# An attention and maxout kernel on one core: two bursts of ones resized and the engines' order searched anew

## The chip, the cores and the metric

The kernel runs on one core of one Trainium2 chip. A core has a matrix engine (TensorE, PE in the profile; its weight loads are PEld), a vector engine (DVE), an activation engine (ACT), a general engine (POOL) and an engine that issues transfers (SP), each with its own queue of instructions that it works off in order. They meet through semaphores alone. The metric is the device time of one execution in microseconds; lower is better.

## What is computed

Queries, keys and values have 8 batches, 8 heads, 1152 positions and 64 channels. Neighbouring queries are averaged in pairs, then comes plain softmax attention, and its output, 4608 tokens of 512 channels, goes through a maxout layer:

```python
q_pool = q.reshape(B, H, S // 2, 2, D).mean(axis=3)
scores = np.matmul(q_pool, k.transpose(0, 1, 3, 2)) / np.sqrt(D)
attn = np.exp(scores - scores.max(-1, keepdims=True))
attn = attn / (attn.sum(-1, keepdims=True) + 1e-09)
x = np.matmul(attn, v).transpose(0, 2, 1, 3).reshape(B * S // 2, H * D)
out = np.maximum(x @ w1, x @ w2) @ w_out
```

## The kernel before

**How the work is cut.** Two heads of one batch make a pair; there are 32 pairs, numbered in order of batch, four to a batch. The scores of all pairs are one long row of 324 groups of 512 columns (`scores`, L665). Each group is computed for both heads at once: a head has 64 channels, so its product uses 64 of the array's 128 rows, and the products of the two heads lie side by side. ACT turns a group into exponentials (L672). A pair's attention times values is a set of products with all 128 rows: first a block of half width for the last 64 queries (L588), then four blocks of nine products for each head (L576). A column of ones next to the values gives the sum of the softmax, so that the normalization is one reciprocal (L598) and two multiplications (L602, L606) on DVE.

The normalized output is transposed, mostly by transfers that SP issues (L712), into `xT`, channels by tokens, in four quarters of the channels, one for each pair of a batch. The maxout layer uses max(a, b) = relu(a - b) + b: the hidden layer (`h_pairs`, L864) multiplies `xT` by w1 - w2 and is cut off at zero by DVE (L874), and the output layer (`p_pair`, L897) adds that times w_out to `xT` times the product of w2 and w_out, which is made once. Both layers use 64-row products in pairs, too. Three forms of product therefore follow each other on TensorE: 64 rows by 128 columns of the array (scores, both layers), 128 by 128 (L576, transposes), and 128 by 64 (L588).

**What sets the order.** The whole program is recorded as a plan of operations with their reads and writes. Five strings give the order on the engines, one character an operation. In `pe_order`, S is the next score group, a digit is the next part of the job in that lane, and the letters U, V, y, z, Y, Z are bursts of products of ones, which compute nothing. `dve_order`, `act_order`, `pool_order` and `sp_order` do the same for the other engines. Whatever the strings say, each operation waits for what it reads and for the buffer that it writes. After score group 21 the scores alternate between two PSUM buffers, and the third one and `fb` serve all other jobs, so a job's bank must be emptied by DVE before the next job on that bank begins.

**The start.** While the first loads are on their way TensorE multiplies ones (`short`, L406): one burst U and six bursts V, then a burst z (`fill`, L397) and then the first transposes of q (L516) and k (L546). DVE adds the first pairs of q (L471), ACT, DVE and POOL convert k (L454, L456, L458). Bursts Y, of 64 rows and 128 columns, stand among the first score groups.

**Later.** q of a later pair goes from POOL (L477) to eight small transposes on DVE (L533), k from POOL (L444) to a transfer that transposes it (L463).

Of the kernel before, what the change touches and what calls it, by code (L numbers as in the profile page):

```python
# [9 lines left out]
P = 128  # L10
# [277 lines left out]
def bass_funnel_attn__then__act_maxout2_kernel(  # L288
# [14 lines left out]
    HP = P // 2  # L303
# [23 lines left out]
    with outer:  # L327
        def sbuf(shape, dt, name):
            return room.enter_context(nc.sbuf_tensor(name, list(shape), dt))
# [5 lines left out]
        ones_tile = sbuf([P, P], BF16, "warm")  # L335
# [32 lines left out]
        fb = [w[:, half, :] for w in wide for half in range(2)]  # L368
# [4 lines left out]
        def rows(half):  # L373
            return slice(half * HP, half * HP + HP)
# [15 lines left out]
            op("POOL", ones, w=["vE0", "vE1", "vE2"])  # L390
            op("DVE", lambda e: e.memset(ones_tile[:, :], 1.0), w=["warm"])

        def fill(m, z):

            def go(e):
                for _ in range(FILL):
                    last = e.matmul(fb[m][:, 384:512], ones_tile[z, :], ones_tile[z, :],  # L397
                                    start=True, stop=True)
                return last
            return m, go  # L400

        def short(m, count, n):

            def go(e):
                for _ in range(count):
                    last = e.matmul(fb[m][0:HP, 384:384 + n], ones_tile[:, 0:HP], ones_tile[:, 0:n],  # L406
                                    start=True, stop=True)
                return last
            return m, go

        FILL = 4
        fills = {"U": short(0, 8, HP), "V": short(1, 10, 52), "y": fill(0, slice(0, P)), "z": fill(1, slice(0, P)),
                 "Y": fill(0, rows(0)), "Z": fill(1, rows(0))}

        def load_k(i, parts=((0, NT),)):
            b, h0, s = i // NHP, 2 * (i % NHP), i % 3
# [500 lines left out]
        def p_job(lo, tail, c0=0, c1=E):  # L917
# [69 lines left out]
        pe_order = (  # L987
            "VUVVVVVz010SS10SzS0SYYSSYYYY0SSS1Y0zS0SSYSY1S1111SSY0S1S01000S1S0SS0677S77S66S66S7S06S70S67S60S0"
            "677SS666S66S000S77S06S000S006S00S06S66667SS000777S00S60S0060S666S666S6000S000S066S66S660S66S1000"
            "S6S1011S666S66S660S000S6766SS6677S07S000S666S666S6666S66110SS010100S66S6666S60S6606S060S060S0000"  # L990
            "S00S67676SS6677S0000S6S0066S660S6666S000S006S666S60S0000SS1111S666S0000S000S066S66S0000SS11011S6"
            "66S6000S0000S0666S666S666S666S66666S0S0000SS1111S666S6666S000S0066606S00666S6000S06S6666SS7777S0"
            "006666S6660600S60S06666S06666000S6666S66S660S000S06667SS66777S000S6666S66S6600S00S6666SS76777S00"
            "S006S66666S66S6666S0066S666S666S666S600S000S6666SS76777S000S00S6666SS767770SS00600S066S6060S6666"
            "00S00S6666S66006S006S0000S6666S0000SS10111S6666S0000S0000666S011SS010100S666S66S6666S666S6666S66"
            "6S660S000S0667SS667767SS00000S00666S0606666S000S6666S666600S0066S6606666S00S6666SS77767S00S000S0"
            "00000S666SS676777S0S006666S666S60S0000S6666S666S600S000S66S6670SS7677S000S006S606S606S666S0110SS"
            "00110S66S6666S6666S66S666S66666S66S66000S00S6666SS67777S00S00000S000S000S000S000S6666SS67777S000"
            "0S60000666S66660000S00066066S66S606000S00006S666S0011SS01100S666S66S60600S0600S0066S66S0000SS011"
            "11S6S600060S000S06666S60000S0000S66S60S00001111S6S666666S660S6666S6060S60S0000S66666S0000S0S6666"  # L1000
            "6SS77770S0066S66S66606S000S00666SS667777SS00666S666660S66S660S6666S066S666S666000S0S06766SS77766"
            "S0000S000S00S00000006266667577174446533104424371124360241400301226275513623301004202513111022050"
            "011372151226260130600511122002507140521113000113100412002013031231216205302022112211523233353335"
# [90 lines left out]
        def k_cuts(i):  # L1094
            return K0 if i == 0 else (0, 5, 9)

        count = {name: len({j for v in jobs_of.values() for j in v.split() if j.split(".")[0] == name})
                 for name in {j.split(".")[0] for v in jobs_of.values() for j in v.split()}}
# [5 lines left out]
        for c in pe_order:  # L1104
# [7 lines left out]
            elif c in fills:  # L1112
                m, fn = fills[c]
                op("PE", fn, r=["warm"], w=[f"f{m}"])
            else:
                m = int(c)
# [30 lines left out]
        dve(lambda e: e.tensor_reduce(flag[0:1, 0:1], badr[0:1, :], AX.X, ALU.max), ["gr"], ["gd4"])  # L1147

        dve_order = (
            "QQ010Q10Q0W0Q100WW111101W10001W077W66667676766WW6666776T6TT06T66T6T776TTTTTTT6T06TTTT001T1006TTT"  # L1150
            "T66T6677TTT0TTTT1010T00TTTT6TTTTTTT666677T6TT60T0T00011T6TT0TTTT0011006TTTT0TTTTTTTTT00T01T106TT"
            "6TTT66T6677TT66TT6TT06TTT666677T0T6TTTTTT666767T0TT6TTTTTT6TT67667TTTT6666776TTTT60TTT60TTTTT000"
            "01160TTT00TTT110T0TT6TTTTTTT66776666TTT60TTTT667676TTTTTTTTT66667766T0T666677TT0T6T1001TTTTTT0TT"
            "0TTT6T667T6T6T7TTTTTTTT0666677T06T060TTTTTTT010001TT0TTTT000011TTT0T60TTTT000011TTTT06T66T66770T"
            "6TTTT6666770T666667706666770302026025170GGGGG026")
        act_order = (
            "CCSSSSSSSSSSSSSSSSSSSSSSSSSSSSSSSSSSSSSSSSSSSSSSSSSSSSSSSSSSSSSSSSSSSSSSSSSSSSSSSSSSSSSSSSSSSSSS"
# [1 line left out]
            "SSSSSSSSSSSSSSSSSSSSSSSSSSSSSSSSSSSSSSSSSSSSSSSSSSSSSSSSSSSSSSSSSSSSSSSSSSSSSSSSSSSSSSSSSSSSSSSS"  # L1159
            "SSSSSSSSSSSSSSSSSSSSSSSSSSSSSSSSSSSSSSSSSSSSSSSSSS125311102134o6o1oo3o5oo")  # L1160
        pool_order = (
            "ivikkvqkvqkkvdqddvqddkqdddvkqkvkvqkkqqvvqqkvvvqkqkqvkqkvqkvvvkqkkqqvqvkkkkvqqvvqvkvqvkqkvqqkkvqv"
            "kvqqvkkvv")
        sp_order = (
            "qkkqwkqwvwqkwwvwwqkkvwwqwvqqwkvwtkkkqvtqkvttkxxkxqvqtxkvxxqqkqqtvoxvxtvooxvxqtqkvqtokxokotkkxoov"
            "xqtxvvxtqovoxtkoxoxkqokotqtvqkvxkqttqvoxooxqkkxxvtxxotqvqovoxvtkoxxvvoxxtkxoxkoqvoxtxqvqxxotvkto"
# [56 lines left out]
```

## Time and profile before

| | us |
|---|---|
| three runs | 363.45, 367.36, 367.65 |
| their median | 367.36 |
| the profiled execution | 364.59 |
| its span, first to last instruction | 363.3 |
| PE busy | 356.7 |
| ACT busy | 314.8 |
| DVE busy | 242.8 |
| POOL busy | 124.4 |

How to read it: the page of the profile gives busy times and the shares of the chain of work that ended last; the chain of waits lists that chain in order of time; the timeline has one row for equal instructions that follow each other without a gap (start, length, engine, line, operation, tiles, shape, how many, and in brackets the idle time before it and what ended it). Matmuls are pipelined: the length of one covers its way through the array, so rows overlap, and what a product costs is read from the start of its row to the start of the next one. Shapes of TensorE are written rows*columns of the array and then rows x columns streamed.

### The profile page before, as it was taken

To read this page: it belongs to the slowest core of one execution; us is meant where nothing else is said; L and a number is where in the kernel's file an instruction comes from. 1 tells how busy PE (TensorE), PEld (TensorE's weight loads), DVE (VectorE), ACT (ScalarE), POOL (GpSimd) and SP (SyncE) were. 2 spreads that over 40 slices of the span, in tenths; PEclk is the share of its full clock that TensorE was granted. 3 is DMA by queue.
4 is the path that set the end of the run, shared out by engine and by line. 5 is a ranking of instruction groups with operands and counts; after the bars stand their busy time and mean duration, and the time that the engine had idled before them with its cause. 6 is when DMAs were issued, how large, how long until landed. Compare 5 with 4: busy or idle time off the path is not lost.

```text
span 363.3 us, 13386 instructions
## 1 busy us (share of the span) xinstructions
PE 356.7 (98%) x5973; PEld 222.6 (61%) x5973; DVE 242.8 (67%) x528; ACT 314.8 (87%) x355; POOL 124.4 (34%) x111
## 2 busy tenths in 40 slices
PE   8999999999999999999999999999999999999995
PEld 6666666566564666656675665666666556666842
DVE  2577688877589767948968594676976846715421
ACT  4999999989999999999989999999999989894221
POOL 1236896424155322552251612623334420010000
PEclk9999999999999999999999999999999999999998
DMA  7999979999969997995999999998999570823115
GB/s 260 403 398 394 394 173 357 240 266 291 327 149 264 303 266 222 249 251 147 271 342 211 246 305 301 261 225 222 231 283 216 166 159 9 196 44 77 33 32 149
DMA packets 77790, 84.78 MB, mean 233 GB/s; under 512 B 50080, under 2 KB 50848, under 8 KB 77728
## 3 DMA queue, kind: packets, MB, share of 16 engines
q1 hardware_dynamic: 77168, 83.09, 86.9%
q8 instruction: 48, 0.79, 0.9%
q10 hardware_dynamic: 560, 0.79, 0.6%
q14 instruction: 14, 0.11, 0.1%
HBM read 62.91 MB, written 9.44 MB: 199 GB/s over the span
## 4 chain that ended last, share of the span: by engine, by line
PE 94%; ACT 4%; DVE 0%; issue 0%; DVEq 0%
PE sps L665 21%; PE sps L576 13%; PE sps L897 11%; PE fb L897 10%; PE sps L864 9%; PE fb L576 7%; PE fb L864 7%; ACT et L672 4%; PE sps L927 3%; PE sps L588 2%; PE fb L789 2%; PE fb L927 1%; PE sps L837 1%; PE fb L588 1%; PE fb L837 1%; PE fb L406 1%
## 5 line engine op out<-in xcount | busy, mean ns | idle before, releaser
L672 ACT ACTIVATE et<-sps 128x1024 bf16<-128x1024 f32 (+1 forms) x336 | 306.6, 1005 | 19.6 <-PE sps L665 17.6
L665 PE MATMUL sps<-qpT,kT 64*128 64x256 bf16 (+7 forms) x1162 | 120.2, 285 | 0.9 <-DVE qpT L523 0.7
L533 DVE STREAM_TRANSPOSE qpT<-qp 32x288 bf16<-32x288 bf16 x216 | 101.4, 469 | 6.7 <-PE sps L665 1.5
L665 PEld LDWEIGHTS sps<-qpT,kT 64*128 64x128 bf16 x1162 | 47.6, 94 | 49.1 <-ACT et L672 16.2
L477 POOL TENSOR_TENSOR qp<-qraw 128x576 bf16<-128x576 f32 x30 | 42.1, 1406 | 90.3 <-DVE qpT L533 60.5
L483 POOL TENSOR_SCALAR vE<-vraw 128x1152 bf16<-128x1152 f32 x32 | 36.9, 1155 | 69.1 <-DMA vraw<-in_v_dram 66.5
L576 PE MATMUL sps<-vE,et 128*128 128x65 bf16 x1440 | 51.4, 193 | 0.0
L576 PEld LDWEIGHTS sps<-vE,et 128*128 128x128 bf16 x1440 | 46.1, 97 | 7.0 <-issue 6.3
L444 POOL TENSOR_SCALAR kbf<-kraw 128x1152 bf16<-128x1152 f32 x31 | 35.7, 1154 | 30.7 <-DMA kraw<-in_k_dram 15.7
L864 PE MATMUL sps<-xT,wd 64*128 64x512 bf16 (+3 forms) x368 | 43.9, 326 | 0.0
L897 PE MATMUL sps<-wo,stage 64*128 64x512 bf16 x256 | 36.8, 376 | 0.0
L874 DVE TENSOR_SCALAR stage<-sps 128x1024 bf16<-128x1024 f32 (+3 forms) x23 | 22.3, 969 | 17.2 <-PE sps L864 17.0
L864 PE MATMUL fb<-xT,wd 64*128 64x512 bf16 (+3 forms) x272 | 33.5, 333 | 0.1
L897 PE MATMUL fb<-wo,stage 64*128 64x512 bf16 x224 | 33.0, 376 | 0.0
L576 PE MATMUL fb<-vE,et 128*128 128x65 bf16 x864 | 30.3, 193 | 0.0
L576 PEld LDWEIGHTS fb<-vE,et 128*128 128x128 bf16 x864 | 27.4, 97 | 4.1 <-issue 3.2
L874 DVE TENSOR_SCALAR stage<-fb 128x1024 bf16<-128x1024 f32 (+3 forms) x17 | 17.0, 999 | 10.7 <-PE fb L864 10.5
L864 PEld LDWEIGHTS sps<-xT,wd 64*128 64x128 bf16 x368 | 15.6, 94 | 12.9 <-PE sps L864 1.1
L598 DVE RECIPROCAL rcs<-sps 128x4 f32<-128x4 f32 (+1 forms) x40 | 7.4, 185 | 18.3 <-PE sps L576 17.7
L897 PE MATMUL sps<-w,xT 64*128 64x512 bf16 x128 | 18.8, 376 | 0.0
L906 DVE COPY stage<-sps 128x1024 f32<-128x1024 f32 x8 | 9.8, 1225 | 12.8 <-PE sps L897 12.7
L897 PEld LDWEIGHTS sps<-wo,stage 64*128 64x128 bf16 x256 | 12.1, 94 | 9.5
(92 smaller groups left out, 295.0 us busy)
## 6 DMA issues: line engine op xcount, KB each, us to landing
vraw<-in_v_dram SPq DMA_DIRECT2D x32, 576.0 KB, 6.6
kraw<-in_k_dram SPq DMA_DIRECT2D x31, 576.0 KB, 6.0
qraw<-in_q_dram SPq DMA_DIRECT2D x31, 576.0 KB, 7.2
out_dram<-stage SPq DMA_DIRECT2D x21, 256.0 KB, 5.6
out_dram<-stage SPq DMA_DIRECT2D x23, 128.0 KB, 3.6
xT<-in_moe_w_dram SPq DMA_DIRECT2D x4, 512.0 KB, 9.7
stage<-in_moe_w_out_dram SPq DMA_DIRECT2D x4, 512.0 KB, 13.6
stage<-in_moe_w_dram SPq DMA_DIRECT2D x4, 512.0 KB, 13.8
```

Of the source, the lines that this page charges most:

```text
L444: op("POOL", lambda g: g.tensor_scalar(kbf[s][:, :, :, :].rearrange("p t h d -> p h t d"), kraw[r][:, :, :, :], 1.0, 1.0, ALU.mult, ALU.mu ...
L477: op("POOL", lambda g: g.tensor_tensor(qpf[s][:, :, :], qraw[r][:, :, 0, :], qraw[r][:, :, 1, :], ALU.add), r=[f"qraw{r}"], w=[f"qp{s}.0", ...
L483: op("POOL", lambda g: g.tensor_scalar(vE[r][:, :, :, 0:D].rearrange("p t h d -> p h t d"), vraw[r][:, :, :, :], 1.0, 1.0, ALU.mult, ALU.m ...
L533: op("DVE", lambda e: e.transpose(view[dst:dst + 32, :, 32 * pb:32 * pb + 32], qpf[s][src:src + 32, :, 32 * db:32 * db + 32]), r=[f"qp{s}. ...
L576: last = e.matmul(fb[m][:, sb * 66:sb * 66 + 65], et[:, a:a + P], vE[vs][:, t, half, 0:65], start=(t == 0), stop=(t == NT - 1))
L588: last = e.matmul(fb[m][rows(half), NCH * 66:NCH * 66 + 65], et[:, a:a + NB], vE[vs][:, t, half, 0:65], start=(t == 0), stop=(t == NT - 1))
L665: last = e.matmul(sps[r][:, h, col:col + hi - lo], kT[i % 3][rows(h), t, :], qpT[i % 3][rows(h), lo:hi], start=True, stop=True)
L672: op("ACT", lambda e: e.activation(et2[:, :, c:c + z - a], sps[r][:, :, a - g * W:z - g * W], EXP, scale=scale), r=[f"s{r}"], w=keys + ([f ...
L864: last = e.matmul(fb[m + k][:, 0:size], wd[z, ct, (f0 + k) * P:(f0 + k + 1) * P], xT[z, ct, n0:n1], start=(turn == 0 and ct == 0), stop=(t ...
L874: dve(lambda e: e.tensor_scalar_max(gT[:, f0:f0 + 2, g0:g0 + size], wide[m // 2][:, :, 0:size], 0.0), [f"f{m}", f"f{m + 1}"], w + [f"f{m}" ...
L897: last = e.matmul(fb[m + k][:, :], lhs, rhs, start=(turn == 0 and j == 0), stop=(turn == 1 and j == NC_ + NF - 1))
L927: return e.matmul(fb[m][:, 0:c1 - c0], lhs, rhs[:, c0:c1], start=(j == 0), stop=(j == NC_ + NF - 1))
```

## The change

The bursts U and V get other sizes: U was eight products of 64 columns and is ten of 64, each V was ten of 52 columns and is eight of 64. The burst Y was four products of 128 columns and is five of 102. The strings of PE, DVE and POOL are other ones from the second batch to the last. ACT's string is as it was, and SP's is too.

```diff
-        def fill(m, z):
+        def fill(m, z, count=4, n=P):
             def go(e):
-                for _ in range(FILL):
-                    last = e.matmul(fb[m][:, 384:512], ones_tile[z, :], ones_tile[z, :],
+                for _ in range(count):
+                    last = e.matmul(fb[m][:, 384:384 + n], ones_tile[z, :], ones_tile[z, 0:n],
                                     start=True, stop=True)
...
-        def short(m, count, n):
+        def short(m, count):
             def go(e):
                 for _ in range(count):
-                    last = e.matmul(fb[m][0:HP, 384:384 + n], ones_tile[:, 0:HP], ones_tile[:, 0:n],
+                    last = e.matmul(fb[m][0:HP, 384:448], ones_tile[:, 0:HP], ones_tile[:, 0:HP],
                                     start=True, stop=True)
...
-        FILL = 4
-        fills = {"U": short(0, 8, HP), "V": short(1, 10, 52), "y": fill(0, slice(0, P)), "z": fill(1, slice(0, P)),
-                 "Y": fill(0, rows(0)), "Z": fill(1, rows(0))}
+        fills = {"U": short(0, 10), "V": short(1, 8), "y": fill(0, slice(0, P)), "z": fill(1, slice(0, P)),
+                 "Y": fill(0, rows(0), 5, 102), "Z": fill(1, rows(0))}
...
-            "S6S1011S666S66S660S000S6766SS6677S07S000S666S666S6666S66110SS010100S66S6666S60S6606S060S060S0000"
+            "S6S1011S666S6666S0000S0S66666SS7777S00S06666S66S6666S66S6666S1066SS0000S66S111S66S6600S0000S000S"
...
-            "kvqqvkkvv")
+            "vvkqqvkkv")
```

The first operations on TensorE before. `warm` is the tile of ones, and the output size is partitions by columns:

```order
L406 MATMUL fb<-warm 64x52 x10
L406 MATMUL fb<-warm 64x64 x8
L406 MATMUL fb<-warm 64x52 x50
L397 MATMUL fb<-warm 128x128 x4
L516 MATMUL fb<-ident,qp 64x64 x8
```

The same place now (the changed file is one line shorter above, so its line numbers are one less from there on):

```order
L406 MATMUL fb<-warm 64x64 x58
L397 MATMUL fb<-warm 128x128 x4
L515 MATMUL fb<-ident,qp 64x64 x8
L545 MATMUL fb<-ident,kbf 128x128 x4
```

Ten products of ones fewer stand ahead of the first transpose of q.

On TensorE near the 124th score group, where the values of one pair (`vE,et`) stand among scores (`qpT,kT`) and the output layer (`wo,stage`), before:

```order
L897 MATMUL fb<-wo,stage 128x512 x2
L588 MATMUL sps<-vE,et 64x65 x18
L665 MATMUL sps<-qpT,kT 128x448 x2
L665 MATMUL sps<-qpT,kT 128x64 x2
L576 MATMUL sps<-vE,et 128x65 x36
L665 MATMUL sps<-qpT,kT 128x512 x4
L576 MATMUL sps<-vE,et 128x65 x36
L665 MATMUL sps<-qpT,kT 128x64 x2
```

And now:

```order
L587 MATMUL sps<-vE,et 64x65 x18
L896 MATMUL fb<-wo,stage 128x512 x4
L664 MATMUL sps<-qpT,kT 128x448 x2
L664 MATMUL sps<-qpT,kT 128x64 x2
L896 MATMUL fb<-wo,stage 128x512 x4
L664 MATMUL sps<-qpT,kT 128x512 x2
L575 MATMUL sps<-vE,et 128x65 x72
L664 MATMUL sps<-qpT,kT 128x512 x2
```

The 72 products stand in one block in place of two, with scores on both sides and none between. Over the whole program the places where one form of product gives way to another, counted in the order, are 216 before and 211 now.

On DVE, where pair 23 is normalized (`xnat`, from the reciprocals `rcs`), among the transposes of a later pair's q (`qpT`), before:

```order
L598 RECIPROCAL rcs<-sps 128x5
L602 TENSOR_TENSOR xnat<-sps,rcs 64x64
L598 RECIPROCAL rcs<-sps 128x4
L533 STREAM_TRANSPOSE qpT<-qp 32x9x32
L602 TENSOR_TENSOR xnat<-sps,rcs 64x64
L533 STREAM_TRANSPOSE qpT<-qp 32x9x32
L606 TENSOR_TENSOR xnat<-sps,rcs 128x4x64
L533 STREAM_TRANSPOSE qpT<-qp 32x9x32
L606 TENSOR_TENSOR xnat<-sps,rcs 128x4x64
```

And now:

```order
L597 RECIPROCAL rcs<-sps 128x5
L601 TENSOR_TENSOR xnat<-sps,rcs 64x64 x2
L605 TENSOR_TENSOR xnat<-sps,rcs 128x4x64
L532 STREAM_TRANSPOSE qpT<-qp 32x9x32
L597 RECIPROCAL rcs<-sps 128x4
L532 STREAM_TRANSPOSE qpT<-qp 32x9x32 x2
L605 TENSOR_TENSOR xnat<-sps,rcs 128x4x64
```

The first head's part is done in one go, and two transposes of q stand between the second head's reciprocal and its end in place of three. On TensorE, between the last product of that pair (L576) and the first product of the hidden layer that reads its channels (L864), there were 38 products of the output layer (L897), 90 products with values and 10 score groups; there are 24, 90 and 8 now.

More of the change, by code (lines that the diff above doesn't have):

```diff
@@ L989, in bass_funnel_attn__then__act_maxout2_kernel @@
             "677SS666S66S000S77S06S000S006S00S06S66667SS000777S00S60S0060S666S666S6000S000S066S66S660S66S1000"
-            "S6S1011S666S66S660S000S6766SS6677S07S000S666S666S6666S66110SS010100S66S6666S60S6606S060S060S0000"
-            "S00S67676SS6677S0000S6S0066S660S6666S000S006S666S60S0000SS1111S666S0000S000S066S66S0000SS11011S6"
-            "66S6000S0000S0666S666S666S666S66666S0S0000SS1111S666S6666S000S0066606S00666S6000S06S6666SS7777S0"
-            "006666S6660600S60S06666S06666000S6666S66S660S000S06667SS66777S000S6666S66S6600S00S6666SS76777S00"
@@ L994, in bass_funnel_attn__then__act_maxout2_kernel @@
[L994 to L998, printed above, removed]
@@ L999, in bass_funnel_attn__then__act_maxout2_kernel @@
-            "0S60000666S66660000S00066066S66S606000S00006S666S0011SS01100S666S66S60600S0600S0066S66S0000SS011"
-            "11S6S600060S000S06666S60000S0000S66S60S00001111S6S666666S660S6666S6060S60S0000S66666S0000S0S6666"
+            "S6S1011S666S6666S0000S0S66666SS7777S00S06666S66S6666S66S6666S1066SS0000S66S111S66S6600S0000S000S"
+            "000S6S6666SS77770S006S0S06666S606S6600S000S06666S6S00000SS1111S6660S000S00S0066S66S0000SS01111S6"
+            "S66600000S000S666S6666S666S66S666S06S0000SS1111S66S6666S660S0000S6666066S6600S600S00S66667777S0S"
@@ new lines, in bass_funnel_attn__then__act_maxout2_kernel @@
+            "00006666S666600S60S006666S666600S6666S6666S0000S0S66666SS7777S0006S666S66S660000S0S66666SS7777S0"
+            "0S6066S6666S066S666S666S666S666S6066S000S00S6766SS66777S00S000S6660SS667777SS0006S0006S0666S6666"
+            "0S00S06666S666S60000S0000S6666S000001SS11166S660000S000S06666S666S0101SS10100S6S6666S66666S666S6"
+            "6S660S000S6767SS77666S00S006666S66606S000S60666S60666S000S6666060S06660S00S06S6667SS6777S000S000"
+            "S0060SS66667777S0S06666S606S066S0000S006S666S666S60000S0S66677SS7667S0000S000S6660S6S6666S000S6S"
@@ L1001, in bass_funnel_attn__then__act_maxout2_kernel @@
+            "111100S666S66S6666S660S060S666S6666S60S66006S00S000S66676SS07677S00S000S0000S000S66666SS7777S000"
+            "0S00006666S66606000S00006666S66S060060S00006S666S0110SS10001S6S66666S00060S60S6000S6666S0000SS01"
+            "111S66S00600S0000S666S60000S000S0666S66S000100111S66S666S660S6666S6060S60S0000S66666S0000S0S6666"
             "6SS77770S0066S66S66606S000S00666SS667777SS00666S666660S66S660S6666S066S666S666000S0S06766SS77766"
@@ L1149, in bass_funnel_attn__then__act_maxout2_kernel @@
         dve_order = (
[L1150 to L1154, printed above, removed]
+            "QQ010Q10Q0W0Q100WW111101W10001W077W66667676766WW6666776T6TT06T66T6T776TTTTTTT6T06TTTT0011006TTT6"
+            "666T77TT0TTTTTTTTTT000TT101TT6TTTT66T66776TTTTT60TT0T00011T60TTT000011T6TTTTTTTT0TTTTT00T0T10T16"
+            "6T66T67766T6TT6T06T6666T77TT06TTTT666677T0TTTTTTTT6TTTTTT6T6T667T7TTTT666677T6TT6060T0000116TTT0"
+            "TTTTTTTT010T1TTT006TTTTT7766666TTTT6TT6TT0TT6T67667TTTT666677TTT6TTT6T0TTT676766TT06TTTTT00011T0"
+            "TTTTTT66666T7TT7T0T66TT67760T60TT60TTTTTT000011T0T000011TTTT0T60TTTTT000011TTTTTTTTT06T66T66770T"
             "6TTTT6666770T666667706666770302026025170GGGGG026")
@@ L1161, in bass_funnel_attn__then__act_maxout2_kernel @@
         pool_order = (
-            "ivikkvqkvqkkvdqddvqddkqdddvkqkvkvqkkqqvvqqkvvvqkqkqvkqkvqkvvvkqkkqqvqvkkkkvqqvvqvkvqvkqkvqqkkvqv"
-            "kvqqvkkvv")
+            "ivikkvqkvqkkvdqddvqddkqdddvkqkkvqkvkqqvvqvkqkkvqvvqkkqqvkvvqvkkqkqqvkvvqkqkkvqkqvqvkvvvkqqkvvqqk"
+            "vvkqqvkkv")
         sp_order = (
```

## The prediction

> **What bounds the kernel now.** I read the page first: its span, the busy times and the shares of the chain that ended last.
>
> ```profile
> span 363.3 us, 13386 instructions
> PE 356.7 (98%) x5973; PEld 222.6 (61%) x5973; DVE 242.8 (67%) x528; ACT 314.8 (87%) x355; POOL 124.4 (34%) x111
> PE 94%; ACT 4%; DVE 0%; issue 0%; DVEq 0%
> ```
>
> TensorE carries 94% of the chain and ACT the 4% that are left. Where each stands is told by the chain of waits of the first 30 us (start, length, what) and by the busy times of three stretches (PE, PEld, DVE, ACT, POOL, then clock and DMA).
>
> ```profile
> 1.11 3.83 PE fb L406 x68
> 4.94 0.54 PE fb L397 x4
> 10.61 0.41 PE sps L665 x4
> 11.04 15.76 ACT et L672 x18
> 26.85 0.47 PE sps L588 x18
> 0.00:20.00 20.00, 17.94 (x296) 12.94 (x296) 9.15 (x18) 14.74 (x17) 5.91 (x14) 1.00 0.92 338
> 40.00:350.00 310.00, 309.85 (x5244) 191.63 (x5239) 216.50 (x475) 278.16 (x313) 108.28 (x90) 1.00 0.89 221
> ```
>
> So the time has three parts. Up to 11.0 us the bursts of ones and the first transposes on TensorE set it, the ones at L406 first of all. From 11.04 to 26.80 the exponentials do. From 26.85 on it is TensorE without a break: 0.15 us idle in the 310 us after 40. A busy matmul row could hide waits, so I checked three neighbours in the timeline:
>
> ```profile
> 121.77 0.81 PE L897 MATMUL sps<-wo,stage 64*128 64x512 bf16 x6
> 122.42 0.38 PE L665 MATMUL sps<-qpT,kT 64*128 64x128 bf16 x4
> 122.63 0.81 PE L897 MATMUL fb<-w,xT 64*128 64x512 bf16 x6
> ```
>
> From start to start six products of the output layer take 0.65 us, 0.108 each, and one score group 0.21 us: two 64-row products side by side over 512 columns. There is no air in that. [...]
>
> ACT is not the second bound by much, though: it waits for scores, all told,
>
> ```profile
> ACT et L672 <- PE sps L665: 17.6, 41, 2.1
> ```
>
> 17.6 us in 41 waits. A TensorE that got over 17 us faster would meet it; this change is far from that.
>
> **The change part by part.** The multiplications of the work itself are the same ones, in another order. What can change is the ones, the switches between forms of product, and waits.
>
> *The bursts.* The rows of the start that matter:
>
> ```profile
> 3.58 0.43 DVE L471 TENSOR_TENSOR qp<-qraw 128x256 bf16<-128x256 f32 x1 [2.52 <-DMA qraw<-in_q_dram]
> 4.87 0.61 PE L397 MATMUL fb<-warm 128*128 128x128 bf16 x4
> 5.41 0.42 PE L516 MATMUL fb<-ident,qp 64*64 64x64 bf16 x8
> 6.34 0.52 POOL L458 TENSOR_SCALAR kbf<-kraw 128x384 bf16<-128x384 f32 x1 [4.82 <-DMA kraw<-in_k_dram]
> 6.86 0.28 DVE L456 CAST kbf<-kraw 128x256 bf16<-128x256 f32 x1
> 7.20 15.86 ACT L672 ACTIVATE et<-sps 128x1024 bf16<-128x1024 f32 x17 [2.10 <-PE sps L665]
> ```
>
> The 68 small products run from 1.11 to 4.87, 55 ns each. The change leaves 58 of 64 columns (before: 60 of 52 and 8 of 64). A 128-column product at 4.87 takes (5.41 - 4.87) / 4 = 135 ns with what follows it; half of that, 68, is the dearest that a 64-column one could be: 58 x 68 = 3.9 us, +0.2. If it costs the same 55 as now, 58 x 55 = 3.2 us, -0.55. I take -0.55: eight of 64 columns are among the 68 already, and a product of half the columns at the dearest is still near the 55. Does it reach the end? The transposes at 5.41 stand behind TensorE's own queue: their input was done at 3.58 + 0.43 = 4.01. They can start 0.55 earlier, at 4.86, and the first exponential too. The next limit is the second piece of K: POOL starts on it at 6.34 as it lands, and DVE's cast of it, now at 6.86, would come at 6.31. So 0.52 of the 0.55 is free, and I count -0.5. If an input lands later, the cover goes and the gain with it: bound 0. What is late next is the exponential chain itself, which then starts 0.5 sooner and runs as before.
>
> *The narrow bursts* (ten of them, four products of 128 columns become five of 102): 512 columns against 510. In this row and the next, 16 products take 0.99 us with the switch, 62 ns each:
>
> ```profile
> 11.72 1.05 PE L397 MATMUL fb<-warm 64*128 64x128 bf16 x16
> 12.71 0.62 PE L765 MATMUL fb<-ident,xT 128*128 128x128 bf16 x8
> ```
>
> If time goes by columns, 0; if by product, 10 x 0.06 = +0.6. It lies beside the exponentials, which pace that stretch. I take 0.
>
> *The switches.* TensorE pays when it goes from one form of product (rows x columns of the array) to another. Around an attention block:
>
> ```profile
> 259.38 0.99 PE L576 MATMUL sps<-vE,et 128*128 128x65 bf16 x27
> 260.31 0.61 PE L665 MATMUL sps<-qpT,kT 64*128 64x256 bf16 x8
> 260.85 1.54 PE L576 MATMUL sps<-vE,et 128*128 128x65 bf16 x45
> 262.32 0.39 PE L665 MATMUL sps<-qpT,kT 64*128 64x384 bf16 x4
> 262.55 0.68 PE L864 MATMUL fb<-xT,wd 64*128 64x256 bf16 x8
> ```
>
> 27 products to the next start: 0.93 us; 45: 1.47. That is 0.030 a product, and 27 x 0.030 = 0.81 leaves 0.12 for going over to scores. Two score groups between attention blocks take 0.54, while one before a product of its own form takes 0.23: 0.54 - 0.46 = 0.08 for going back. So 0.10 a switch. Counted along the order there are 216 switches before and 211 after: 5 x 0.10 = -0.5. Bounds: 0, if a switch falls beside a wait, and 5 x 0.12 = -0.6.
>
> *Waits.* Those that the old order had are worth at most the 0.15 us idle, so nothing to win. What can be lost is a new one, and the nearest place is where pair 23 is finished. Its second half must be normalized on DVE, sent through SP's transposes and landed before the hidden layer reads it at 262.55:
>
> ```profile
> 253.23 0.39 PE L665 MATMUL sps<-qpT,kT 64*128 64x384 bf16 x4
> 253.33 0.18 DVE L598 RECIPROCAL rcs<-sps 128x4 f32<-128x4 f32 x1 [0.64 <-PE sps L576]
> 253.53 0.47 DVE L533 STREAM_TRANSPOSE qpT<-qp 32x288 bf16<-32x288 bf16 x1
> 254.26 1.14 SPq L712 DMA_TRANSPOSE xT<-xnat  x1
> 255.44 1.66 SPq L463 DMA_TRANSPOSE kT<-kbf  x1
> 255.68 0.42 DVE L606 TENSOR_TENSOR xnat<-sps,rcs 128x256 bf16<-128x256 f32 x1
> 257.14 1.42 SPq L712 DMA_TRANSPOSE xT<-xnat  x1
> xT<-xnat SPq DMA_TRANSPOSE x1, 5.8
> ```
>
> It lands at 257.14 + 5.8 = 262.9. The block begins at 262.55, and its first product on that quarter of the channels is the seventh, six times 0.054 (half of 0.108, for half the columns) later, at 262.87: no slack at all. In the new order 14 output products and two score groups fewer stand between: 14 x 0.108 + 2 x 0.21 = 1.9 us less. Part comes back: DVE now has two transposes of q among the halves instead of three, and the last half ends 1.6 us after the block (0.18 + 2 x 0.47 + 0.42) where it ended 256.10 - 253.2 = 2.9 after. That leaves 0.6 later. SP's two issues ahead (1.14 and 1.66) took 1.0 us beyond the norm's end and still do in part. Bounds: 0 (the landing was set by the queue's backlog and stays at 262.9) and 1.9; I take +0.5, near the 0.6.
>
> Sum: -0.5 (ones) - 0.5 (switches) + 0.5 (transposes) = -0.5 us; ends -1.1 and +2.1 (the one with no wait at the transposes and the switches at their dearest, the other with the ones at +0.2, the switches at 0 and the wait at 1.9).
>
> **The level.** The profiled execution took 364.59 us (span 363.3 and 1.3 around it); by its own time the sum gives 364.1. The runs shown are 363.45, 367.36 and 367.65, so it lies with the low one, and the median of 367.36 with the high ones. Nothing in one trace tells which a later run will be. I take the mean of all four, 365.8, and forecast 365.3.
>
> **The rivals.**
>
> *The transposes come too late (slower).* The whole 1.9 us at pair 23 is waited for, since SP is in order and its latency there was 5.8 us; TensorE stands, and scores behind it with it. -1.0 + 1.9 = +0.9: 366.7. It decides as soon as that wait is over 1.0 us. For it: zero slack now. Against: DVE's new order gives back 1.3.
>
> *The clock opens later (slower).* At the start TensorE runs at half rate although the clock column shows 1.00: the same four products of ones,
>
> ```profile
> 8.87 0.61 PE L397 MATMUL fb<-warm 128*128 128x128 bf16 x4
> 15.39 0.40 PE L397 MATMUL fb<-warm 128*128 128x128 bf16 x4
> ```
>
> take 0.61 and then 0.40. [...] If it opens some 3 us later, TensorE's work from the row at 10.61 to the end of the one at 12.71, 2.7 us, would take twice as long; its idle time in the first 20 us, 20 - 17.94 = 2.1, takes up some of that, so between 0.6 and 2.7, of which I take +2.0: 365.3 + 2.0 = 367.3. Against: the row at 8.87 stands 7.8 us after the first product and is still slow with all of the old ones ahead of it, so their number is not what opens the clock. One chance in ten. [...]
>
> *Nothing arrives.* The second K piece lands 0.5 later than in this trace, the ones gain nothing: 0 - 0.5 + 0.5 = 0, 365.8.
>
> [...]
>
> **How the numbers follow.** Forecast 0.45; late transposes 0.20; clock later 0.10; nothing 0.10; faster 0.15. What a run is worth moves more than the cases do: the lowest run less 1.5 is 362.0, the highest with 0.9 is 368.6, and 362.0 to 368.6 holds 8 in 10. About 2% can be told from no change here, 7.3 us on 367.36. No case comes near it in either direction; only something that I have not seen does. Faster by over 2%: 0.05, within 0.91, slower 0.04.
>
> **What would show it.** The ones end near 4.3 us and the first exponential starts near 6.7, the fifth near 10.5: first term right. PE idle in 40 to 350 stays under 0.5: second and third. A PE row at L864 near 262 that starts with a wait for a transpose of xT, or score waits of ACT well over 17.6 us, shows the late transposes. Slow products of ones after 11 us show the clock. An exponential chain that breaks between 11 and 27, or DVE waits that show up before TensorE anywhere after 60 us, would make the prediction wrong altogether.

## The result and the profile after

The changed kernel takes 366.36 us, the median of 22 runs (364.91 to 369.7), against 364.31 (22 runs, 363.1 to 368.55) for the kernel before in the same comparison. The ratio is 1.0055, with a 95% interval from 1.0032 to 1.0078: about 2 us slower, less than the 2% that counts here, but the interval leaves out 1. The time lies in the forecast's range of 362.0 to 368.6; the direction was wrong, -0.5 us forecast and +2 found. About three in ten executions of the kernel before lie some 3 us above its others; the medians and ratios here contain them.

The profiled execution of after took 366.5 us. Its lines of code have numbers one lower than in the kernel before (L896 is the output layer that was L897). The page, as quoted of before:

```profile
span 365.3 us, 13378 instructions
PE 354.7 (97%) x5969; PEld 220.7 (60%) x5973; DVE 244.0 (67%) x528; ACT 313.8 (86%) x355; POOL 124.5 (34%) x111
PE 87%; ACT 5%; DMA 3%; DVE 1%; issue 1%; POOL 1%; SPq 0%; DVEq 0%; POOLq 0%
```

TensorE has fallen from 94% of the chain to 87%, and transfers, DVE, POOL and "issue" (a wait that nothing in the profile explains) have come into it. The chain of the first 30 us and the busy times of four stretches say where:

```profile
1.73 5.14 DMA kraw<-in_k_dram
...
6.95 0.62 POOL kbf L457
...
7.96 0.37 PE sps L664 x4
...
8.35 17.59 ACT et L671 x20
...
25.99 0.47 PE sps L587 x18
```

```profile
40.00:350.00 310.00, 306.87 (x5221) 189.32 (x5221) 216.69 (x472) 275.97 (x311) 108.01 (x89) 1.00 0.88 221
80.00:90.00 10.00, 8.28 (x144) 4.78 (x142) 8.14 (x22) 8.05 (x9) 4.38 (x4) 1.00 1.11 290
130.00:140.00 10.00, 8.86 (x143) 5.06 (x140) 6.41 (x16) 7.63 (x9) 2.52 (x2) 1.00 1.16 323
250.00:270.00 20.00, 20.00 (x376) 13.14 (x372) 12.54 (x28) 18.62 (x22) 3.67 (x3) 1.00 0.99 231
```

The start is better: the products at L587 that close the exponentials' part begin at 25.99, where they began at 26.85 (L588). But from 40 to 350 us TensorE, the second figure of a row, is idle for 3.13 us and no longer for 0.15: 1.72 between 80 and 90, 1.14 between 130 and 140. At the place that the prediction feared, 250 to 270, it is not idle at all. TensorE's own waits:

```profile
PE fb L896 <- DVE xnat L605: 1.7, 1, 1.7
PE fb L896 <- issue: 1.1, 1, 1.1
```

**The first gap** is read from the timeline around it, of POOL, of DVE and of TensorE in turn:

```profile
78.03 1.40 POOL L476 TENSOR_TENSOR qp<-qraw 128x576 bf16<-128x576 f32 x1 [5.44 <-DMA qraw<-in_q_dram]
```

```profile
79.54 0.95 DVE L532 STREAM_TRANSPOSE qpT<-qp 32x288 bf16<-32x288 bf16 x2 [3.37 <-POOL qp L476]
80.50 0.19 DVE L597 RECIPROCAL rcs<-fb 128x5 f32<-128x5 f32 x1
80.73 0.46 DVE L601 TENSOR_TENSOR xnat<-fb,rcs 64x64 bf16<-64x64 f32 x2
81.22 0.95 DVE L532 STREAM_TRANSPOSE qpT<-qp 32x288 bf16<-32x288 bf16 x2
82.18 0.18 DVE L597 RECIPROCAL rcs<-fb 128x4 f32<-128x4 f32 x1
82.39 0.76 DVE L605 TENSOR_TENSOR xnat<-fb,rcs 128x256 bf16<-128x256 f32 x2
```

```profile
80.89 0.59 PE L896 MATMUL sps<-wo,stage 64*128 64x512 bf16 x4
83.20 0.60 PE L896 MATMUL fb<-w,xT 64*128 64x512 bf16 x4 [1.72 <-DVE xnat L605]
```

DVE stood from 76.17 to 79.54 before two transposes of q, because POOL had to scale that q and POOL waited for its load. Behind these two transposes in DVE's queue stood a normalization whose first half could have begun sooner, two more transposes divided its halves, and its last step let go of the bank that TensorE's next product writes. From start to start the two rows of TensorE are 2.31 us apart where four such products take 0.43: 1.88 us are lost.

**The second gap** has no releaser:

```profile
131.59 0.81 PE L896 MATMUL fb<-w,xT 64*128 64x512 bf16 x6
133.54 0.39 PE L896 MATMUL fb<-wo,stage 64*128 64x512 bf16 x2 [1.14 <-issue]
```

1.95 us from start to start, where six products take 0.65: 1.30 lost.

ACT's order is the same in all kernels here, so the starts of its exponentials are common milestones. Column by column: the kernel before, the changed one, the changed one again, and kernels of the experiments below (all in us).

| exponential | before | after | after again | normalization first | bursts alone | fewer loads |
|---|---|---|---|---|---|---|
| 1st | 7.20 | 6.35 | 6.45 | 6.67 | 6.32 | 6.30 |
| 19th | 23.78 | 22.92 | 22.86 | 23.09 | 22.73 | 22.71 |
| 81st | 81.75 | 80.44 | 80.62 | 81.02 | 80.70 | 80.33 |
| 91st | 91.69 | 92.26 | 92.52 | 91.17 | 90.65 | 92.25 |
| 321st | 315.16 | 317.00 | 316.40 | 314.71 | 313.90 | 316.02 |

At the 321st, after is 1.84 behind: -0.86 from the start, +1.88 and +1.30 from the two gaps make +2.32, and -0.48 is left for everything else.

### The profile page after: what moved, and what is told of

Its sections match the earlier page's. It is cut to its first block, busy times and chain, and to the rows that moved or that the text cites. A ratio compares the mean times of both kernels' runs of the same rounds, so it can differ in the third digit from the quotient of the medians.

```text
span 365.3 us, 13378 instructions
## 1 busy us (share of the span) xinstructions
PE 354.7 (97%) x5969; PEld 220.7 (60%) x5973; DVE 244.0 (67%) x528; ACT 313.8 (86%) x355; POOL 124.5 (34%) x111
## 3 DMA queue, kind: packets, MB, share of 16 engines
q1 hardware_dynamic: 77168, 83.09, 85.5%
## 4 chain that ended last, share of the span: by engine, by line
PE 87%; ACT 5%; DMA 3%; DVE 1%; issue 1%; POOL 1%; SPq 0%; DVEq 0%; POOLq 0%
PE sps L664 19%; PE sps L575 13%; PE fb L896 10%; PE sps L896 10%; PE sps L863 8%; PE fb L575 7%; PE fb L863 6%; ACT et L671 5%; PE sps L926 3%; PE sps L587 2%; PE fb L788 2%; DMA qraw<-in_q_dram 2%; PE fb L926 1%; DMA kraw<-in_k_dram 1%; PE sps L836 1%; PE fb L836 1%
## 5 line engine op out<-in xcount | busy, mean ns | idle before, releaser
L863 PE MATMUL sps<-xT,wd 64*128 64x512 bf16 (+3 forms) x368 | 43.0, 326 | 0.0
L896 PE MATMUL sps<-wo,stage 64*128 64x512 bf16 x256 | 37.0, 376 | 0.0
L896 PE MATMUL fb<-wo,stage 64*128 64x512 bf16 x224 | 34.3, 376 | 1.1 <-issue 1.1
L896 PE MATMUL fb<-w,xT 64*128 64x512 bf16 x112 | 17.9, 377 | 1.7 <-DVE xnat L605 1.7
L896 PE MATMUL sps<-w,xT 64*128 64x512 bf16 x128 | 18.3, 377 | 0.0
L863 PEld LDWEIGHTS fb<-xT,wd 64*128 64x128 bf16 x272 | 11.9, 94 | 10.2 <-PE fb L863 2.2
```

The costliest lines, as they stand in the source:

```text
L863: last = e.matmul(fb[m + k][:, 0:size], wd[z, ct, (f0 + k) * P:(f0 + k + 1) * P], xT[z, ct, n0:n1], start=(turn == 0 and ct == 0), stop=(t ...
L896: last = e.matmul(fb[m + k][:, :], lhs, rhs, start=(turn == 0 and j == 0), stop=(turn == 1 and j == NC_ + NF - 1))
```

## The experiments

**The bursts alone, the orders alone, and one queue mended.** The first kernel has the new bursts and the old strings, the second the new strings and the old bursts:

```diff
-        fills = {"U": short(0, 8, HP), "V": short(1, 10, 52), "y": fill(0, slice(0, P)), "z": fill(1, slice(0, P)),
-                 "Y": fill(0, rows(0)), "Z": fill(1, rows(0))}
+        fills = {"U": short(0, 10), "V": short(1, 8), "y": fill(0, slice(0, P)), "z": fill(1, slice(0, P)),
+                 "Y": fill(0, rows(0), 5, 102), "Z": fill(1, rows(0))}
```

> The kernel before with the changed bursts of ones (58 products of 64 columns, narrow ones of 102) and the old orders. Theory 'orders': the bursts gain what the trace of after shows at the start, the score groups past the first exponentials beginning at 25.99 instead of 26.85, so 0.5 to 0.9 us faster than the kernel before, and TensorE stays without a break, under 0.5 us idle from 40 to 350. Rival 'bursts': the ones are what costs the 2 us (a clock that opens late, or a later phase of everything behind), then this kernel is 1.5 to 2.5 us slower than the one before.

> The changed kernel with the old bursts. Theory 'orders': slower than the kernel before by 2.5 to 3 us, the whole of what after lost plus the 0.86 it won at the start; TensorE waits at L896 near 82 us for a normalization on DVE (1.7 us there) and perhaps near 133 (1.1 to 1.5). Rival 'bursts': within 0.5 us of the kernel before, and neither wait is there.

The bursts alone took 363.52 us (before: 364.44), ratio 0.9983, interval 0.995 to 1.0017. TensorE is idle for 0.17 us from 40 to 350, and the products that end the exponentials' part begin at 25.79. The rival, 1.5 to 2.5 us slower, is out; that the bursts gain is not shown by this interval, which holds 1. The orders alone took 366.71, ratio 1.0037, interval 1.0001 to 1.0073: slower, by 2.3 us in the medians and 1.3 by the ratio, where 2.5 to 3 were expected. Their trace missed part of the expectation: no wait at 82 us, and 0.29 of "issue" at 135. In that execution the granted clock went back to a half from 7.8 to 18.0 us, so that the 19th exponential came at 27.25, 4.3 later than in after, while POOL started on the q in question only 2.4 later (80.44). DVE's order there was the same, transposes first; TensorE was just late enough not to notice. So this execution suggests that the wait depends on how far TensorE runs ahead of the loads; it does not tell how often the other executions of this kernel had it.

The third kernel is the changed one with this edit in DVE's string (T is a transpose of q, the digits are the normalization's steps):

```diff
-            "666T77TT0TTTTTTTTTT000TT101TT6TTTT66T66776TTTTT60TT0T00011T60TTT000011T6TTTTTTTT0TTTTT00T0T10T16"
+            "666T77TT0TTTTTTTT000101TTTTTT6TTTT66T66776TTTTT60TT0T00011T60TTT000011T6TTTTTTTT0TTTTT00T0T10T16"
```

> The changed kernel with one edit in DVE's order: the four transposes of q that stand before and between the two halves of a normalization near 80 us come behind it. Theory 'place in the queue': the normalization (0.19 + 2 x 0.23 + 0.18 + 2 x 0.42 = 1.67 us) starts as the attention block ends near 80.0 and not after two transposes of 0.47 that waited for q; its end moves from 83.2 to about 81.8, TensorE's wait at L896 from 1.7 to about 0.4, and the time is 1.0 to 1.5 us less than that of the changed kernel. Rival 'late load': the wait is made by q's load and stays over 1 us whatever DVE does first, or comes back at once at the scores that need q; the time is within 0.4 of the changed kernel.

It took 364.44, ratio to before 0.9992 (0.9955 to 1.0029): 1.9 us less than the median of the changed kernel, more than the 1.0 to 1.5 expected, and 1.3 less than the one run of the changed kernel on the same chip (365.71, below). Its trace has no gap at 132 either, so part of the 1.9 may be that one. The stretch of the mended wait alone, from the 81st to the 91st exponential in the table, took 11.82 us in after, takes 10.15 here, and took 9.94 before. The timeline of its DVE and the row of TensorE at that place:

```profile
78.75 0.19 DVE L597 RECIPROCAL rcs<-fb 128x5 f32<-128x5 f32 x1 [1.99 <-PE fb L575]
78.98 0.46 DVE L601 TENSOR_TENSOR xnat<-fb,rcs 64x64 bf16<-64x64 f32 x2
80.69 0.18 DVE L597 RECIPROCAL rcs<-fb 128x4 f32<-128x4 f32 x1 [1.26 <-PE fb L575]
80.91 0.76 DVE L605 TENSOR_TENSOR xnat<-fb,rcs 128x256 bf16<-128x256 f32 x2
81.58 2.86 DVE L532 STREAM_TRANSPOSE qpT<-qp 32x288 bf16<-32x288 bf16 x6
```

```profile
81.90 0.59 PE L896 MATMUL fb<-w,xT 64*128 64x512 bf16 x4
```

The first half is now done while TensorE works on the second, DVE waits for TensorE and not the other way round, and the wait is gone, not merely shorter. The transposes of q come some 2 us later, and no score waits for them; TensorE only waits 0.22 us at 85.5 for a copy of DVE's that now stands behind them. POOL started on the q in question at 78.40, no sooner than in after (78.03), so the load was as late as there. With the same late load, the place in the queue makes the wait; and as the orders alone showed, the place makes it only where TensorE is early enough.

**The fault put into the old order.** The counter-test: the bursts alone, with three transposes moved ahead of the normalization in the old string.

```diff
-            "T66T6677TTT0TTTT1010T00TTTT6TTTTTTTT666677T6TT60T0T00011T6TT0TTTT0011006TTTT0TTTTTTTTT00T01T106TT"
+            "T66T6677TTT0TTTTTTT101000TT6TTTTTTTT666677T6TT60T0T00011T6TT0TTTT0011006TTTT0TTTTTTTTT00T01T106TT"
```

> The kernel before with the changed bursts, and one edit in DVE's order: three transposes of q, two of which wait for POOL's scaling of q near 79.6 us, are moved ahead of the normalization near 77 (they stood inside and behind it). Theory 'place in the queue': the normalization (0.18 + 0.19 + 0.42 + 0.21 + 0.23 + 0.42 = 1.65 us) can only start at 79.6 + 2 x 0.47 = 80.6 and ends near 82.3; the first products of L896 that need its bank stood at 79.72 and wait some 2.5 us; the time is 1.8 to 2.8 us over that of the kernel with the bursts alone (363.5), so about 365.8. Rival 'only the new order of TensorE is short there': the old order takes it up, the wait stays under 0.8 us and the time under 364.5.

It took 365.65 us, 2.04 over the bursts alone on the same chip (363.61), ratio to before 1.0042 (1.0009 to 1.0075). The time is in the expected band. The wait was 1.67 us and not 2.5, as POOL was ready half a microsecond sooner than reckoned and the six steps took 1.46:

```profile
79.05 0.95 DVE L532 STREAM_TRANSPOSE qpT<-qp 32x288 bf16<-32x288 bf16 x2 [3.58 <-POOL qp L476]
```

```profile
81.53 0.39 PE L896 MATMUL fb<-w,xT 64*128 64x512 bf16 x2 [1.67 <-DVE xnat L605]
```

The stretch from the 19th to the 81st exponential, in which this wait lies, is 59.68 us long for 57.97 with the bursts alone, 1.71 more, and no gap ends on "issue" in either trace. So the same fault costs about the same in either order of TensorE.

**The second gap.** First, the changed kernel once more:

> The changed kernel once more, for the gap of 1.5 us on TensorE at 132.0 that no semaphore of the profile explains. Theory 'place': the same gap of 1.0 us or more stands before the same two products of L896, because the instructions of TensorE's own stream reach it late there, in every execution. Rival 'accident of one execution': no gap over 0.5 us between 125 and 140, and the wait at 82 us is there unchanged (1.4 to 1.9).

It took 365.71 us. The wait at 82 is there (1.80; 2.39 from start to start), and the other gap is smaller, but before the same two products. Neither expectation fits whole: it is under the 1.0 us of the first, and no accident of one execution:

```profile
PE fb L896 <- DVE xnat L605: 1.8, 1, 1.8
PE fb L896 <- issue: 0.3, 1, 0.3
```

The page has a queue of instructions (the row "q8 instruction: 48, 0.79, 0.9%"), 48 packets of 16 KB. TensorE has some 12000 instructions in the trace (in after 5969 matmuls and 5973 weight loads), about 250 for each packet, so it is taken that these are TensorE's; that one packet brings 256 is read from the table below. If TensorE ran out of them, the gap must follow the count of instructions and not the product. So the stream was shifted: ten narrow bursts of ten products of 51 columns, 100 instructions more ahead of everything.

```diff
-                 "Y": fill(0, rows(0), 5, 102), "Z": fill(1, rows(0))}
+                 "Y": fill(0, rows(0), 10, 51), "Z": fill(1, rows(0))}
```

> The changed kernel with each of the ten narrow bursts of ones as ten products of 51 columns in place of five of 102: the same columns, 50 products and so 100 instructions more ahead of everything in TensorE's stream, 0.39 of the 256 instructions that one transfer of the instruction queue brings. Theory 'late instructions': the gap near 132 (1.5 us in the first trace of after, 0.3 in the second, before the same two products of L896, each time with the 17th transfer of that queue landing later than 1.5 transfers' worth of instructions behind) is tied to where the stream is cut, so it is gone from those products, and if there is another it stands 50 products away from them or at another transfer. Rival 'something at those products' (weights, a bank of the accumulator): the gap of 0.3 to 1.5 us stands before the same products again. Both: the wait at 82 us is there, 1.4 to 1.9 us, and the time is 364.5 to 367.

> The same kernel as the one before it, for a second trace, since the gap varied between two traces of after. Theory 'late instructions': again nothing over 0.15 us before those two products of L896. Rival: 0.3 us or more there.

368.52 and 368.61 us, 1.5 over the upper end of what was expected. The wait at 82 was 2.3 us in the first trace, over the 1.4 to 1.9 expected, and 1.7 in the second. Nothing waits near 132 any more. Instead there are gaps of the same kind at other places, two of them the same in both traces, here of the first:

```profile
PE fb L397 <- issue: 1.7, 1, 1.7
PE sps L664 <- issue: 0.7, 1, 0.7
```

```profile
19.91 0.18 PE L397 MATMUL fb<-warm 64*128 64x51 bf16 x1
21.80 0.39 PE L397 MATMUL fb<-warm 64*128 64x51 bf16 x9 [1.70 <-issue]
```

```profile
197.52 0.38 PE L664 MATMUL sps<-qpT,kT 64*128 64x64 bf16 x3
198.55 0.35 PE L664 MATMUL sps<-qpT,kT 64*128 64x448 bf16 x1 [0.65 <-issue]
```

They cut a burst of ten equal products behind its first, and a score group of four behind its third, where nothing is waited for in the program. Counted in the trace, the instructions of TensorE ahead of every such gap are these. The count takes in matmuls, weight loads and the 7 to 48 semaphore and drain instructions that the trace has among them; without these the last column would run from 145 to 187. A few instructions may be missing from a trace.

| trace | gap at, us | idle, us | instructions ahead | of them behind the last full 256 |
|---|---|---|---|---|
| after | 132.4 | 1.14 | 4547 | 195 |
| after again | 132.7 | 0.31 | 4547 | 195 |
| orders alone | 135.0 | 0.29 | 4547 | 195 |
| before, a second trace | 131.3 | 0.51 | 4547 | 195 |
| shifted | 20.1 | 1.70 | 706 | 194 |
| shifted | 197.9 | 0.65 | 6849 | 193 |
| shifted again | 20.1 | 0.59 | 706 | 194 |
| shifted again | 94.1 | 0.25 | 3266 | 194 |
| shifted again | 196.8 | 1.11 | 6849 | 193 |
| fewer loads (below) | 205.0 | 0.22 | 7105 | 193 |

Always the same place in a block of 256: in the second trace of the shifted kernel 2560 instructions lie between the first gap and the second, ten times 256, and 6143 between the first and the third, 24 times 256 less one. The times of the packets fit as well: in each of the ten gaps TensorE's next product starts 1.2 to 1.5 us after the end of the packet whose number is the count of full blocks ahead (the 17th for 4547). Over all fourteen traces, 644 packets, the instruction at this place never starts sooner than 1.23 us after the end of its packet, gap or no gap. The old order ran dry at the same instruction as the new one, before another product (a hidden layer's), so these gaps belong to neither order.

Then, why that block is late. In after its packet ran from 131.0 to 132.0, just as a stretch of transfers at about 400 GB/s ended. The test cuts six loads to two ninths of their bytes (this part of the result is left out):

```diff
+                    later(f"lk{i}", old("ck", i, 3), lambda i=i: load_k(i, ((0, 2 if i in (14, 15) else NT),)))
+                    later(f"lq{i}", old("cq", i, 3), lambda i=i: load_q(i, ((0, 2 if i in (15, 16, 17) else QU),)))
...
+            n = 2 if i == 13 else NT
...
+                v[b, h0:h0 + 2, :, :].rearrange("h (p t) d -> p h (t d)", t=NT)[:, :, 0:n * D]),
```

> The changed kernel with six loads of Q, K and V, those that SP issues between about 114 and 129 us, cut to two ninths of their bytes (the pairs behind them are computed from older data in the same buffers, so this part of the result is left out; the arithmetic is as long as before). TensorE ran dry at the same cut of its stream, near 132, in three traces of the new orders, and the 17th transfer of its instructions landed at 131.0, 130.6 and 132.9 there, as the DMA engines ended a stretch of about 400 GB/s. Theory 'the loads are in the way': with some 2.7 MB less that transfer lands two us or more sooner, less than 1.45 transfers' worth of instructions behind, and no gap stands near 132. Rival 'it is asked for late whatever the traffic': it lands 1.5 to 1.7 behind again, with a gap of 0.3 to 1.5 us. The wait at 82 us is before all this and stays.

The packet ran from 128.1 to 129.0, 2.9 us sooner. When it began, TensorE had started 1.06 blocks of instructions beyond the sixteenth (after: 1.67), and the two products follow the six before them without a gap (this kernel has the line numbers of before):

```profile
131.58 0.81 PE L897 MATMUL fb<-w,xT 64*128 64x512 bf16 x6
132.22 0.38 PE L897 MATMUL fb<-wo,stage 64*128 64x512 bf16 x2
```

0.64 us from start to start, against 1.95. The wait at 82 stayed (1.8), the time was 365.42. This fits the loads being in the way of TensorE's own instructions, but one execution does not show it: the kernel with the normalization first had all its loads, its packet ran from 128.8 to 129.8 (1.41 blocks), and it had no gap there either. And in this kernel a gap of 0.22 us came at 205.0, where the loads are whole (last row of the table). How the transfers take turns is not shown by this.

**The bursts again, and the spread of the kernel before.**

> The kernel before with the changed bursts alone, timed once more for a narrower interval: 58 products of 64 columns end at 4.34 us where 68 ended at 4.87, so 0.5 us are expected, ratio 0.9985; if the clock's opening is what moved in the first trace (5.12 us against 9.67), it varies by itself and the ratio is within 0.999 to 1.001.

363.61 us, ratio 0.9963, interval 0.993 to 0.9996 (before: 364.04). With the first comparison (0.9983), the bursts alone are faster than the kernel before by some 0.6 to 1.3 us by these ratios, of which only the second interval, and narrowly, leaves out 1. Their medians are the lowest of the study. The profiled execution of this run took 365.82: its clock opened at 6.61 us, was back at a half from 10.03 to 16.85, and the 19th exponential came at 25.94, later than in the first trace of before. So the new bursts do not keep a start from being late.

> The kernel before, for the spread of its times: most lie between 363 and 364.6 us, a third at 366.7 to 367.9. In the first trace (363.3) TensorE's full clock began at 9.67 us, in the traces with the changed bursts at 4.0 to 7.0. Theory 'start': a run of the upper group shows the clock opening one step of 3.41 us later, at about 13, and the first exponentials some 3 us later, with all the rest as in the lower group; a run of the lower group opens at 9.7 or before. Rival 'a stall later on': the upper group has its 3 us in a gap behind 30 us.

> The same kernel and the same question as the run before it: time over 366.5 us with the clock opening at about 13 us or a stall behind 30 us, or a time of 363 to 364.6 with neither.

> The same kernel and question once more: time over 366.5 us with the clock opening at about 13 us or a stall behind 30 us, or a time of 363 to 364.6 with neither.

364.36, 364.31 and 367.20 us: the third was of the upper group. Ones of the trace of before and of this one, where the same burst of sixteen takes 1.05 and 1.91 us:

```profile
11.72 1.05 PE L397 MATMUL fb<-warm 64*128 64x128 bf16 x16
...
14.66 0.39 PE L397 MATMUL fb<-warm 64*128 64x128 bf16 x4
```

```profile
12.95 1.91 PE L397 MATMUL fb<-warm 64*128 64x128 bf16 x16
...
17.71 0.39 PE L397 MATMUL fb<-warm 64*128 64x128 bf16 x4
```

Its full clock begins at 17.56 us by the trace's records of the clock, the others' at 9.78 and 10.24. The 19th exponential comes at 26.84, 3.06 later than in the first trace, the 321st 2.60 later, and TensorE is idle for 0.30 us from 40 to 350. "Start" holds, though the clock came later still than the 13 us guessed.

## Why the prediction was right and wrong

*What bounds the kernel.* Right. TensorE from 27 us on is what counts, and what it lost there came out at the end nearly whole. In the counter-test a wait of 1.67 us that was put into the old order on TensorE cost 2.04 at the end.

*The ones, -0.5.* Right in kind and a little small. They ended at 4.34 (forecast 4.3), 55.7 ns each; the first exponential began at 6.35 (6.7) and the fifth at 10.17 (10.5). At the 19th 0.7 to 1.3 us were won in seven of the nine traces with the new bursts, and not 0.5. The clock opened sooner as well: at 4.0 to 7.0 us in all nine (in one it closed again, from 10.03 to 16.85, and 2.2 us were lost; another lost 0.25 with a dry stream at 20.1), at 9.7 to 17.6 in four of five with the old ones (in the fifth at 4.4, to close again as well). That the sooner clock brings what is over the 0.5 fits these traces: with the opening at 4.02 us the 19th came at 22.50, at 5.21 at 22.92, at 6.97 at 23.09, at 9.67 at 23.78. No run moved the clock alone. The rival "the clock opens later" had the sign the wrong way round in all traces but the one that closed again. The limit named next, the second piece of K, is in the chain of after as foretold.

*The narrow bursts, 0.* Right: five products of 102 columns take 45 ns each, the old four of 128 took 56.

*The switches, -0.5.* Not settled. -0.48 is left over in after, and -0.2 to -0.5 in the other traces of the new orders, which would fit (the two with the shifted stream, with more products of ones, lie above before by the same reckoning); but between traces of the one old order the same stretch differs by up to 0.46 without any change.

*Waits, +0.5 at pair 23.* This is the step that failed, and in two ways. "The nearest place is where pair 23 is finished": no wait came there, and not for the reason that the "against" had given. These are the last half of that normalization, SP's issue of its transpose, its time to landing, and the hidden layer that reads it:

```profile
259.50 0.42 DVE L605 TENSOR_TENSOR xnat<-sps,rcs 128x256 bf16<-128x256 f32 x1
260.75 1.57 SPq L711 DMA_TRANSPOSE xT<-xnat  x1
xT<-xnat SPq DMA_TRANSPOSE x1, 2.9
264.46 0.60 PE L863 MATMUL fb<-xT,wd 64*128 64x256 bf16 x8
```

The block of values ends at 257.11, so TensorE's way from there to the hidden layer is 7.35 us long for 9.32 before, 2.0 less where 1.9 was reckoned. DVE's way is not shorter: its last half ends 2.8 us after the block, as before (2.9), and not 1.6. The transfer made up for it: it landed 2.9 us after its issue, at 263.6, where 5.8 had been needed before. Why it was quicker is open, so that this place cost nothing is luck. The wait came at 82 us instead and cost 1.88. The second failure is that "what can be lost is a new one" was followed up only there, where TensorE's slack against SP's transposes was zero. The order showed DVE's transposes of q moved ahead of a normalization elsewhere, and the trace of before showed POOL standing 5.08 us for a load of q at 78.9: a transpose that waits for such a load holds everything behind it in the queue. Both were to be seen, and were not put side by side. The text had said what would prove it wrong "altogether", DVE waits that show up before TensorE anywhere after 60 us, and that is what happened.

*What was not foreseen at all* is the dry instruction stream, 1.30 us in the profiled execution. As it comes in the old order too (0.51 in one of four traces), and not in every trace of the new one, how much of it the change brings is open.

*The sum and the level.* -0.5 against about +2.0. The level of 365.8, a mean of four executions, was 1.5 too high for the kernel before (medians 364.0 to 364.4 of 22 to 29 runs), so by luck it took 1.5 off the change's error of 2.5, and the 365.3 came out 1.1 under the 366.36 measured. The upper executions are real, but three in ten; the one of them that was traced owes its time to the clock at the start.

## What to carry to other kernels

When a search moves steps of an in-order engine, go through the queue for every step that waits for a load and has been put ahead of a step that frees a buffer of the bottleneck: its price is the wait that is queued, not the 0.47 us that it takes itself. A gain that was put together with a reordering should be timed alone: here the bursts were worth 0.2 to 0.4% by their ratios, hardly more than the noise, and the strings lost at least as much. And where a saturated TensorE shows gaps that end on "issue", count the instructions ahead of them before looking for a dependency.

## What the runs showed of the hardware

The clock at the start moves in steps: by the trace's records the granted clock was at a half for 10.24 us in the orders alone and for 6.83 in one trace of the bursts alone, three and two times 3.413, and full for 351.57 us in before and 358.40 in after, 103 and 105 times that. The phase differs from execution to execution: the full clock begins at 9.67, 9.78, 10.24 and 17.56 us in the four traces of before. What opens it is not shown. In the first trace of before TensorE was busy for 3.35 of the 3.42 us from 2.84 to 6.26, and the full clock began one step later, at 9.67; in the trace with the fault put in it began at 4.02, behind a step in which TensorE was busy for 2.91 us. That it opens later with the old bursts because their products are narrower is the author's guess: nine openings at 4.0 to 7.0 us with the new ones and four at 9.7 to 17.6 with the old ones speak for it, and one at 4.38 with the old ones against it.

TensorE's instructions can come late: it ran dry for 0.22 to 1.70 us in seven of the fourteen traces, each time at the same place in a block of 256, and went on 1.2 to 1.5 us after the end of a packet of its instruction queue. That a dense stretch of loads holds these packets up is the author's guess, from the traffic of 400 GB/s just ahead of the one at 131.0; no run shows it by itself.
